# The last pair's first two products interleaved, an opening rewritten, and when the corner sums run

## The chip, the cores and the metric

The kernel runs on one core of a Trainium2 chip. The metric is the device time of one execution in microseconds (us); lower is better. The engines are named as the profile names them: PE (TensorE; PEld is its weight load), DVE (VectorE), ACT (ScalarE), POOL (GpSimd), SP (SyncE, here only a DMA queue).

## The reference

A decayed linear attention over 4 batches, 8 heads, 768 positions and head size 64, in fp32, feeds a feed-forward layer on 3072 tokens:

```python
# per block of 64 positions (the kernel uses 128, which is the same function)
intra = (qb @ kb^T) * Dmask            # Dmask[i, j] = lam^(i-j) for i >= j, else 0
out   = intra @ vb + (qb * lam^(i+1)) @ kv_state
kv_state = lam^block * kv_state + (kb * lam^(block-1-j))^T @ vb
# then, on x = out as [3072 tokens, 512]
h = x @ w_in                           # 512 -> 2048
g = where(h > 0, h, exp(min(h, 0)) - 1)   # ELU
y = g @ w_out                          # 2048 -> 512
```

## The kernel before

**Tiling.** A block g is 128 positions of one batch; there are 24 (6 chunks in time x 4 batches, g = 4 x chunk + batch). Blocks 0 to 3 stand alone; from 4 on they go in pairs (4 and 5, up to 22 and 23), named by the first. Per block the attention has these steps, each a letter of the order that is written out by hand: `T` transposes q and k (on PE with copies by DVE and ACT; from block 8 on with DMA transposes on SP), `S` the scores, whose mask is multiplied in on DVE as two `pp` tiles, `P` the block's output (psO, copied to xt), `U` the update of the state, `z`/`Z` its zeroing, `M` the decay of the old state (stt), `W` the transposes, `kd` (the decayed keys, on POOL) and `M` of a later block together.

**The feed-forward.** `1:g:j` (function `mm1`) is one block of the first product: 8 or 16 matmuls into one of two psH banks, then exp and relu on ACT and later one instruction on DVE (L640) that makes g, the ELU, and so frees the psH bank. `2:g:j` (function `mm2`) is a plain second product. From pair 8 on the second product of a pair is done with seven products instead of eight, M1 to M7, as in Strassen's scheme: `7:g:i` (function `mm2_seven`) runs them in the order M3, M4, M5, M2, M1, M7, M6, each 8 matmuls of 256 columns, one for each pair of slices of the 2048. Their operands are the g tiles themselves (gg; M3 and M4), sums of gg's quarters (fp for M5 and M2, fe for M1, fd for M7 and M6; function `sums`, L497 on POOL or L500 on DVE as `SHARED` says) and sums of w_out (wf; functions `w_sums`, `F` on DVE and `G` on POOL). M3, M5, M1 and M6 write one psM bank of the pair, M4, M2 and M7 the other (M5 adds onto M3's half, M2 onto M4's, M6 onto M1's); the next pair takes the two banks the other way round. The products are combined at the corners: ACT copies M3 and M4 out (L558), POOL adds them (t, L594), ACT copies M5 and M2 out (L569), POOL makes u (L605) and s2 (L565), DVE adds M1 to u (w1, also L565), and DVE makes the last two quarters of the output with M7 and M6 (osb, L582). The last pair's output is stored in four pieces, each as soon as it is there.

**What sets the order.** The program's order is each engine's order. Until pair 6 it is the string `OPEN`; POOL's loads and other work of that time follow `POOL_ORDER` (q, k, v, i and o are loads of q, k, v, w_in and w_out, d is kd, m is M). After that, a loop puts one `1:` block after the other and between them the seven products of the pair before and, at fixed offsets (`AT`), the attention of the pair to come; `LAGU` says how far behind plain second products may fall before they go two at a time. `BANKS` gives the PSUM banks of single steps; two names are two banks. DVE's work is deferred through lists: `pending` (the g of the last `1:` block), `late` (masks, state updates, corner sums), `slow` (the sums of gg) and `later` (the osb of M7 and M6). `flush`, called at the head of every product, emits the pending g, then at most one of `late` and of `slow`, then what is due in `later`:

```python
while later and later[0][0] <= 0:
    later.pop(0)[1]()
```

In `mm2_seven` the products 2, 4 and 5 first empty `slow`; product 6 first empties `late` until w1 is made.

Of the kernel before, what the change touches and what calls it, by code (L numbers as in the profile page):

```python
# [11 lines left out]
ALU = mybir.AluOpType  # L12
# [3 lines left out]
def kernel(  # L16
# [11 lines left out]
    nc = tc.nc  # L28
# [3 lines left out]
    L = 128  # L32
# [14 lines left out]
        "q1 k0 iota k2 k1 q2 v0 v1 i0 i1 v2 i3 i2 o0 o1 d0 k3 q3 i4 i5 d1 o2 d2 o3 d3 o4 v3 o5 "  # L47
        "i6 i7 k4 o7 o6 q4 k6 m4 v4 q6 d5 d4 q8 q10 k8 d6 v6 v8 d7 v10 k10 m6"
# [11 lines left out]
    )  # L60
    LAGU = 13
    LATE = 4
    MACT = 12
    DELAY = 0
# [3 lines left out]
    SHARED = {8: 'D', 10: 'ED', 12: 'ED', 14: 'ED', 16: '', 18: '', 20: '', 22: 'ED'}  # L68
    AT = {'L': -19, 'l': 1, 'W': -13, 'T': -5, 'S': -7, 'B': -5}
    BANKS = (  # L70
        "S0=M0,A S1=D,C S2=D,M1 S3=D,B P0=M1 P1=M0 P2=B P3=A U0=B U1=B U2=B U3=M1 T0=M1,D "
        "T1=D,C T2=M0,D T3=B T4=B T5=D T6=M1 T7=D M2=C M3=M0"
# [449 lines left out]
    def mm2_seven(g0, i):  # L522
        flush()
        while slow and i in (2, 4, 5):
            slow.pop(0)()
# [4 lines left out]
        while i == 6 and "w1" not in z:  # L530
            late.pop(0)()
# [8 lines left out]
        out = z["bank1" if m in (4, 2, 7) else "bank0"][:, half]  # L540
        for s in range(NFT // 2):
            t = g2[(g0, s // 2)]
            p, d, e = forms[(g0, s // 2)]
            u = s % 2
            lhs = {3: t[:, u, 0, 0, :], 4: t[:, u, 1, 1, :], 1: e[:, u, :], 7: d[:, u, 1, :],
                   6: d[:, u, 0, :], 5: p[:, u, 0, :], 2: p[:, u, 1, :]}[m]
            if m in (5, 2):
                rhs = wo16[s][:, 1, R_] if m == 5 else wo16[s][:, 0, L_]
            else:
                rhs = wf[s][:, (3, 4, 1, 6, 7).index(m), :]  # L550
            nc.tensor.matmul(  # L551
                out, lhsT=lhs, rhs=rhs, start=(s == 0 and m in (3, 4, 1, 7)),
                stop=(s == NFT // 2 - 1), skip_group_check=True,
            )

        def keep(n):
            z[n] = msb.tile([128, 256], FP32, tag=n, bufs=1, name=f"{n}_{g0}")
            nc.scalar.copy(out=z[n][:], in_=out)  # L558
# [13 lines left out]

        last = g0 == NG - 2
# [15 lines left out]
        if m == 3:  # L589
            keep("m3")  # L590
        elif m == 4:
            keep("m4")
# [15 lines left out]
        elif m == 2:  # L608
            corner(1, L_)
            if COMB is nc.vector:  # L610
                late.insert(0, lambda: comb("s2", "t", None, ALU.subtract))
            else:
                comb("s2", "t", z[1][:, L_], ALU.subtract)
        elif m == 1:
            late.insert(0, lambda: comb("w1", "u", None, ALU.add, nc.vector))
        elif m == 7:
            last_of(0, L_, "w1", ALU.subtract)
        else:
            last_of(1, R_, "s2", ALU.add)
# [6 lines left out]
    def flush():  # L626
        while pending:
# [19 lines left out]
            if g0 in SEVEN and j % 2 == 1:  # L647
                slow.extend(sums(g0, j // 2))
        if late:
            late.pop(0)()  # L650
        if slow and len(late) < 2:
            slow.pop(0)()
# [211 lines left out]
```

## Time and profile before

| | us |
|---|---|
| median of 14 runs | 213.59 |
| lowest and highest of them | 213.07, 214.87 |
| the profiled execution's own time | 214.82 |
| its span, first to last instruction | 213.1 |
| PE busy in it | 197.6 (93%) |
| POOL, DVE, ACT busy | 160.2, 159.2, 137.9 |
| M1 to M7 of a pair, each | 0.87 from the first matmul to the next product's |

In the lines of a timeline the columns are start, duration, engine, source line, operation, output<-inputs, shapes and count; the brackets give the idle time of the engine just before and what ended it. Matmuls are pipelined: eight of 256 columns that take 1.03 to the end of the last let the next start after 0.87. DVE's and ACT's instructions overlap their neighbours by some 0.1 us. In the chain of waits the columns are start, duration and what ran.

### The profile page before, as it was taken

Reading aid. Unit: us, or ns where it says so; the run is one execution under the profiler, and the core shown is the slowest. Engines: PE = TensorE matmul, PEld = TensorE weight load, DVE = VectorE, ACT = ScalarE, POOL = GpSimd, SP = SyncE. Lnnn points to the kernel's source line nnn. Section 1 sums busy time; section 2 is a strip of 40 time slices with the busy share of each in tenths; the row PEclk is TensorE's granted clock in tenths of the full one; section 3 lists DMA queues with packets and bytes.
Section 4 is the critical chain, followed back from the end, with each engine's and each line's share of the span. In section 5 each row is a group of like instructions: output and inputs, shape, how many; then the busy total and the mean of one; then the engine's idle time right before and its main releaser. Section 6 shows DMA issues by size and latency. Waiting matters only on the chain.

```text
span 213.1 us, 5654 instructions
## 1 busy us (share of the span) xinstructions
PE 197.6 (93%) x2224; PEld 158.2 (74%) x2224; DVE 159.2 (75%) x294; ACT 137.9 (65%) x277; POOL 160.2 (75%) x187
## 2 busy tenths in 40 slices
PE   0679999999999999999999999999999999999983
PEld 0459676777676676667887887887988878888862
DVE  3864382579975968989978879879989889886522
ACT  4535664883876675866966966867567667577630
POOL 7999599999999999597999999996361201206961
PEclk9999999999999999999999999999999999999998
DMA  8999999999993030999959959979999611011032
GB/s 88 135 172 185 197 169 174 166 177 195 134 186 87 3 98 3 123 168 143 136 84 158 121 87 154 117 95 152 111 119 179 101 52 49 3 49 49 3 115 82
DMA packets 102122, 24.61 MB, mean 116 GB/s; under 512 B 92624, under 2 KB 99280, under 8 KB 102096
## 3 DMA queue, kind: packets, MB, share of 16 engines
q0 software_dynamic: 79760, 13.50, 83.3%
q1 hardware_dynamic: 22336, 10.76, 27.2%
q8 instruction: 17, 0.28, 0.6%
q14 instruction: 9, 0.07, 0.2%
HBM read 27.27 MB, written 6.29 MB: 158 GB/s over the span
## 4 chain that ended last, share of the span: by engine, by line
PE 69%; DVE 8%; DMA 7%; ACT 7%; POOL 5%; issue 2%; SPq 0%; ACTq 0%; POOLq 0%; DVEq 0%
PE psH L674 31%; PE psM L551 20%; PE psM L699 10%; DMA wo<-in_moe_w_out_dram 5%; ACT e L680 3%; ACT psH L681 3%; PE psS L304 3%; DVE gg L640 2%; DMA kT<-kn 2%; PE psO L340 2%; DVE g L640 2%; PE psO L346 1%; POOL wi L149 1%; POOL vn L107 1%; POOL kn L107 1%
## 5 line engine op out<-in xcount | busy, mean ns | idle before, releaser
L674 PE MATMUL psH<-xt,wi 128*128 128x256 f16 (+1 forms) x896 | 101.5, 262 | 2.5 <-DVE gg L640 1.2
L674 PEld LDWEIGHTS <-wi 128*128 128x128 f16 x896 | 79.4, 100 | 17.7 <-issue 4.0
L680 ACT ACTIVATE e<-psH 128x512 f32<-128x512 f32 x96 | 57.3, 597 | 48.7 <-PE psH L674 47.7
L681 ACT ACTIVATE psH<-psH 128x512 f32<-128x512 f32 x96 | 57.0, 593 | 0.0
L640 DVE SCALAR_TENSOR_TENSOR gg<-e,psH 128x512 f16<-128x512 f32 x64 | 43.7, 683 | 16.5 <-ACT psH L681 16.2
L640 DVE SCALAR_TENSOR_TENSOR g<-e,psH 128x512 f16<-128x512 f32 x32 | 21.9, 684 | 18.1 <-ACT psH L681 17.9
L320 DVE TENSOR_TENSOR pp<-psS,mask 128x512 f16<-128x512 f32 x48 | 31.4, 683 | 3.8 <-PE psS L304 3.8
L699 PE MATMUL psM<-wo,g 128*128 128x512 f16 x128 | 32.1, 379 | 0.5 <-DMA wo<-in_moe_w_out_dram 0.5
L176 POOL TENSOR_TENSOR kd<-kn,ks 128x512 f16<-128x512 f16 x20 | 21.0, 1055 | 5.6 <-DMA kn<-in_k_dram 5.5
L497 POOL TENSOR_TENSOR fd<-gg 128x512 f16<-128x512 f16 x20 | 24.3, 1216 | 0.1
L517 POOL TENSOR_TENSOR wf<-wo 128x256 f16<-128x256 f16 (+1 forms) x28 | 21.1, 794 | 0.2
L497 POOL TENSOR_TENSOR fe<-gg 128x256 f16<-128x256 f16 x16 | 11.8, 735 | 12.0 <-DVE gg L640 11.9
L594 POOL TENSOR_TENSOR t<-m,m 128x256 f32<-128x256 f32 x8 | 5.9, 736 | 18.3 <-ACT m L558 18.3
L699 PEld LDWEIGHTS <-g 128*128 128x128 f16 x128 | 11.7, 98 | 10.3 <-issue 0.8
L551 PE MATMUL psM<-wf,gg 128*128 128x256 f16 x128 | 16.8, 273 | 0.8 <-DVE osb L582 0.5
L551 PE MATMUL psM<-wo,fp 128*128 128x256 f16 x128 | 16.5, 273 | 0.0
L551 PE MATMUL psM<-wf,fd 128*128 128x256 f16 x128 | 16.4, 273 | 0.0
L107 POOL DMA_DIRECT2D qn<-in_q_dram x13 | 14.8, 1136 | 0.9 <-POOLq L848 0.8
L107 POOL DMA_DIRECT2D kn<-in_k_dram x14 | 15.3, 1096 | 0.0
L107 POOL DMA_DIRECT2D vn<-in_v_dram x14 | 15.3, 1098 | 0.0
L500 DVE TENSOR_TENSOR fp<-gg 128x512 f16<-128x512 f16 x32 | 14.6, 456 | 0.6
L551 PEld LDWEIGHTS <-gg 128*128 128x128 f16 x128 | 11.9, 98 | 3.2 <-issue 0.7
(62 smaller groups left out, 250.4 us busy)
## 6 DMA issues: line engine op xcount, KB each, us to landing
out_dram<-osb SPq DMA_DIRECT2D x22, 256.0 KB, 2.6
kn<-in_k_dram POOLq DMA_DIRECT2D x10, 256.0 KB, 6.5
qn<-in_q_dram POOLq DMA_DIRECT2D x10, 256.0 KB, 6.0
vn<-in_v_dram POOLq DMA_DIRECT2D x10, 256.0 KB, 8.4
wi<-in_moe_w_in_dram POOLq DMA_DIRECT2D x8, 256.0 KB, 7.8
wo<-in_moe_w_out_dram POOLq DMA_DIRECT2D x8, 256.0 KB, 9.5
kn<-in_k_dram POOLq DMA_DIRECT2D x4, 128.0 KB, 4.2
vn<-in_v_dram POOLq DMA_DIRECT2D x4, 128.0 KB, 5.6
```

What stands on the lines that cost most here:

```text
L107: nc.gpsimd.dma_start(out=t[:].rearrange("p b h d -> p (b h) d"), in_=src)
L176: nc.gpsimd.tensor_tensor(out=kd[:], in0=of(kg, g), in1=ks[:].unsqueeze(2).broadcast_to([128, H, 64]), op=ALU.mult,)
L320: nc.vector.tensor_tensor(out=P[:], in0=pts[hh][:], in1=mask[:, hh::2, :], op=ALU.mult)
L497: nc.gpsimd.tensor_tensor(out=out[:], in0=in0, in1=in1, op=op)
L500: lambda out=out, in0=in0, in1=in1, op=op: nc.vector.tensor_tensor(out=out[:], in0=in0, in1=in1, op=op)
L517: eng.tensor_tensor(out=out, in0=in0, in1=in1, op=op)
L551: nc.tensor.matmul(out, lhsT=lhs, rhs=rhs, start=(s == 0 and m in (3, 4, 1, 7)), stop=(s == NFT // 2 - 1), skip_group_check=True,)
L640: nc.vector.scalar_tensor_tensor(out=g.rearrange("p f c t -> p (f c t)"), in0=e[:], scalar=-1.0, in1=r[:], op0=ALU.add, op1=ALU.min,)
L674: nc.tensor.matmul(pH[:, f * n * 128 : (f + 1) * n * 128], lhsT=wi16[i][:, kk, w * 128 : (w + 1) * 128], rhs=xg[g0][:, kk, :], start=(kk = ...
L680: nc.scalar.activation(e[:], pH[:], AF.Exp)
L681: nc.scalar.activation(pH[:], pH[:], AF.Relu)
L699: nc.tensor.matmul(psM[g][:, cols], lhsT=gts[(g, j * FB + f)], rhs=wo16[i][:, w, cols], start=first and f == 0, stop=end and f == FB - 1, ...
```

## The change

- In `mm2_seven`, of the last pair (22): M3 runs 7 of its 8 matmuls as product 0. Product 1 begins with `SPLIT` = 3 matmuls of M4, then M3's last and its copy by ACT, then M4's other five.
- The osb of the pair ahead is emitted before the last g: product 6 of pair 20 calls no `flush`, and product 0 of pair 22 first empties `later`.
- `slow` holds its pair beside each entry, and products 2, 4 and 5 empty only what belongs to their own pair.
- w1 is emitted with M1 and no longer put in `late`.
- `SHARED`: pair 8's fe goes from DVE to POOL (four instructions).
- `OPEN`, `POOL_ORDER`: steps change places. `BANKS`: T1's second half goes to bank D, where its first is, and no longer to C. `LAGU` is 14 instead of 13 and T's offset -7 instead of -5.

On PE the built order differs in these places only: T3 ahead of 1:0:1, S3 ahead of 1:0:2, U2 ahead of 1:3:2, 1:4:2 ahead of S6 and S7, and the last pair's M3 and M4. On DVE, the masks of S6 go behind the g of 1:4:3, the fe of pair 8 are gone, in each pair one state update goes ahead of the second fp and w1 ahead of fe and fd, and at the end the osb of pair 20's M6 goes ahead of the last g. On SP one store goes behind the two transposes of block 10.

```diff
@@ -44,32 +44,33 @@
     WI = [2] * 8
     WO = [2] * 8
     POOL_ORDER = (
-        "q1 k0 iota k2 k1 q2 v0 v1 i0 i1 v2 i3 i2 o0 o1 d0 k3 q3 i4 i5 d1 o2 d2 o3 d3 o4 v3 o5 "
-        "i6 i7 k4 o7 o6 q4 k6 m4 v4 q6 d5 d4 q8 q10 k8 d6 v6 v8 d7 v10 k10 m6"
+        "q1 k0 iota k2 k1 q2 v0 v1 i0 i1 v2 i3 i2 o0 d0 o1 k3 q3 i4 i5 d1 o2 d2 o3 d3 o4 v3 o5 "
+        "i6 i7 k4 o7 o6 q4 k6 m4 v4 q6 d5 d4 q10 k8 q8 d6 v6 d7 v8 v10 m6 k10"
     )
     RAW = "q0"
     FIRST = "q0:0 c0 c1 c2"
     OPEN = (
-        "z3 z0 z1 Z2 Z1 z2 Z0 T0 T1 S0 S1 T2 P0 P1 S2 1:0:0 U0 1:1:0 P2 1:1:1 1:2:0 2:0:0 "
-        "1:2:1 2:1:0 1:0:1 T3 2:2:0 1:0:2 S3 1:2:2 2:2:1 U1 1:1:2 2:1:1 2:0:1 P3 2:0:2 1:3:0 "
-        "2:1:2 1:1:3 M 1:2:3 Z3 2:2:2 1:3:2 U2 1:3:1 2:1:3 1:0:3 T4 T5 2:2:3 1:3:3 S4:5 2:3:0 "
-        "2:0:3 2:3:2 U3 F0 B:P4:P5:U4:U5 M 2:3:3 1:4:1 T6 1:4:0 G3 T7 2:3:1 G4 W9 1:4:3 G5 G1 "
-        "S6:7 1:4:2 G2 2:5:0 2:4:0 1:4:4 1:4:5 W8 B:P6:P7:U6:U7 1:4:7 1:6:1 2:5:1 2:4:1 G7 "
-        "1:4:6 1:6:0 G6 2:4:2 S8:9 1:6:2 1:6:4 2:5:2 2:5:3 W11 1:6:3 1:6:6 B:P8:P9:U8:U9 1:6:7 "
-        "2:4:3 1:6:5 W10 L12"
+        "z1 z0 Z1 z3 z2 Z2 Z0 T0 T1 S0 S1 T2 P0 P1 S2 1:0:0 U0 1:1:0 P2 1:1:1 1:2:0 2:0:0 "
+        "1:2:1 2:1:0 T3 1:0:1 2:2:0 S3 1:0:2 1:2:2 2:2:1 U1 1:1:2 2:1:1 2:0:1 P3 2:0:2 1:3:0 "
+        "2:1:2 1:1:3 1:2:3 Z3 2:2:2 U2 1:3:2 1:3:1 M 2:1:3 1:0:3 T4 T5 2:2:3 1:3:3 S4:5 2:3:0 "
+        "2:0:3 2:3:2 U3 F0 B:P4:P5:U4:U5 M 2:3:3 1:4:1 T6 1:4:0 G3 T7 2:3:1 G4 W9 1:4:3 G1 G5 "
+        "1:4:2 S6:7 2:5:0 2:4:0 G2 1:4:4 1:4:5 W8 B:P6:P7:U6:U7 1:4:7 1:6:1 2:5:1 2:4:1 1:4:6 "
+        "G7 1:6:0 G6 2:4:2 S8:9 1:6:2 1:6:4 2:5:2 2:5:3 W11 1:6:3 1:6:6 B:P8:P9:U8:U9 1:6:7 "
+        "2:4:3 W10 1:6:5 L12"
     )
-    LAGU = 13
+    LAGU = 14
     LATE = 4
     MACT = 12
+    SPLIT = 3
     DELAY = 0
     COMB = nc.gpsimd
 
     SEVEN = (8, 10, 12, 14, 16, 18, 20, 22)
-    SHARED = {8: 'D', 10: 'ED', 12: 'ED', 14: 'ED', 16: '', 18: '', 20: '', 22: 'ED'}
-    AT = {'L': -19, 'l': 1, 'W': -13, 'T': -5, 'S': -7, 'B': -5}
+    SHARED = {8: 'ED', 10: 'ED', 12: 'ED', 14: 'ED', 16: '', 18: '', 20: '', 22: 'ED'}
+    AT = {'L': -19, 'l': 1, 'W': -13, 'T': -7, 'S': -7, 'B': -5}
     BANKS = (
         "S0=M0,A S1=D,C S2=D,M1 S3=D,B P0=M1 P1=M0 P2=B P3=A U0=B U1=B U2=B U3=M1 T0=M1,D "
-        "T1=D,C T2=M0,D T3=B T4=B T5=D T6=M1 T7=D M2=C M3=M0"
+        "T1=D,D T2=M0,D T3=B T4=B T5=D T6=M1 T7=D M2=C M3=M0"
     )
     TAGS = {w: t.replace(",", " ") for w, t in (x.split("=") for x in BANKS.split())}
 
@@ -520,15 +521,18 @@
     later, sides = [], [0, 1]
 
     def mm2_seven(g0, i):
-        flush()
-        while slow and i in (2, 4, 5):
-            slow.pop(0)()
+        last = g0 == NG - 2
+        if last and i == 0:
+            while later:
+                later.pop(0)[1]()
+        if g0 != NG - 4 or i < 6:
+            flush()
+        while i in (2, 4, 5) and any(x[0] == g0 for x in slow):
+            slow.pop(0)[1]()
         if i == 0:
             seven[g0] = {}
             sides.reverse()
         z = seven[g0]
-        while i == 6 and "w1" not in z:
-            late.pop(0)()
         if i < 2:
             while later:
                 later.pop(0)[1]()
@@ -537,25 +541,47 @@
             )
         m = (3, 4, 5, 2, 1, 7, 6)[i]
         half = L_ if i < 4 else R_
-        out = z["bank1" if m in (4, 2, 7) else "bank0"][:, half]
-        for s in range(NFT // 2):
-            t = g2[(g0, s // 2)]
-            p, d, e = forms[(g0, s // 2)]
-            u = s % 2
-            lhs = {3: t[:, u, 0, 0, :], 4: t[:, u, 1, 1, :], 1: e[:, u, :], 7: d[:, u, 1, :],
-                   6: d[:, u, 0, :], 5: p[:, u, 0, :], 2: p[:, u, 1, :]}[m]
-            if m in (5, 2):
-                rhs = wo16[s][:, 1, R_] if m == 5 else wo16[s][:, 0, L_]
-            else:
-                rhs = wf[s][:, (3, 4, 1, 6, 7).index(m), :]
-            nc.tensor.matmul(
-                out, lhsT=lhs, rhs=rhs, start=(s == 0 and m in (3, 4, 1, 7)),
-                stop=(s == NFT // 2 - 1), skip_group_check=True,
-            )
-
-        def keep(n):
+
+        def place_of(m):
+            return z["bank1" if m in (4, 2, 7) else "bank0"][:, half]
+
+        def keep(m):
+            n = f"m{m}"
             z[n] = msb.tile([128, 256], FP32, tag=n, bufs=1, name=f"{n}_{g0}")
-            nc.scalar.copy(out=z[n][:], in_=out)
+            nc.scalar.copy(out=z[n][:], in_=place_of(m))
+
+        def terms(m, slices):
+            for s in slices:
+                t = g2[(g0, s // 2)]
+                p, d, e = forms[(g0, s // 2)]
+                u = s % 2
+                lhs = {3: t[:, u, 0, 0, :], 4: t[:, u, 1, 1, :], 1: e[:, u, :],
+                       7: d[:, u, 1, :], 6: d[:, u, 0, :], 5: p[:, u, 0, :],
+                       2: p[:, u, 1, :]}[m]
+                if m in (5, 2):
+                    rhs = wo16[s][:, 1, R_] if m == 5 else wo16[s][:, 0, L_]
+                else:
+                    rhs = wf[s][:, (3, 4, 1, 6, 7).index(m), :]
+                nc.tensor.matmul(
+                    place_of(m), lhsT=lhs, rhs=rhs,
+                    start=(s == 0 and m in (3, 4, 1, 7)),
+                    stop=(s == NFT // 2 - 1), skip_group_check=True,
+                )
+
+
+        end = NFT // 2
+        if last and i == 0:
+            terms(3, range(end - 1))
+            return
+        if last and i == 1:
+            terms(4, range(SPLIT))
+            terms(3, [end - 1])
+            keep(3)
+            terms(4, range(SPLIT, end))
+        else:
+            terms(m, range(end))
+        out = place_of(m)
+
 
         def comb(n, x, y, op, eng=COMB):
 
@@ -587,9 +611,9 @@
 
 
         if m == 3:
-            keep("m3")
+            keep(3)
         elif m == 4:
-            keep("m4")
+            keep(4)
             z["t"] = msb.tile([128, 256], FP32, tag="t", bufs=1, name=f"t_{g0}")
             nc.gpsimd.tensor_tensor(
                 out=z["t"][:], in0=z["m3"][:], in1=z["m4"][:], op=ALU.add
@@ -612,7 +636,7 @@
             else:
                 comb("s2", "t", z[1][:, L_], ALU.subtract)
         elif m == 1:
-            late.insert(0, lambda: comb("w1", "u", None, ALU.add, nc.vector))
+            comb("w1", "u", None, ALU.add, nc.vector)
         elif m == 7:
             last_of(0, L_, "w1", ALU.subtract)
         else:
@@ -645,11 +669,11 @@
                 for c in range(n):
                     gts[(g0 + c, j * (FB // n) + f)] = g[:, f, c, :]
             if g0 in SEVEN and j % 2 == 1:
-                slow.extend(sums(g0, j // 2))
+                slow.extend((g0, x) for x in sums(g0, j // 2))
         if late:
             late.pop(0)()
         if slow and len(late) < 2:
-            slow.pop(0)()
+            slow.pop(0)[1]()
         for x in later:
             x[0] -= 1
         while later and later[0][0] <= 0:
```

More of the change, by code (lines that the diff above doesn't have):

```diff
@@ L571, in corner @@
                 store(c, half)
-        last = g0 == NG - 2
         def store(c, cols):
```

## The prediction

> **What bounds the kernel now.** I read the page's busy shares first, then the chain that ended last, then the timelines at the places that the diff touches. The share and the chain both say TensorE:
>
> ```profile
> PE 197.6 (93%) x2224; PEld 158.2 (74%) x2224; DVE 159.2 (75%) x294; ACT 137.9 (65%) x277; POOL 160.2 (75%) x187
> PE 69%; DVE 8%; DMA 7%; ACT 7%; POOL 5%; issue 2%; SPq 0%; ACTq 0%; POOLq 0%; DVEq 0%
> ```
>
> From 99 to 191 us TensorE does the same 15.5 us per pair over and over, with one gap of 0.37 us in each (PE waits for a g to free a psH bank; the chain there is exp, relu, g). A change pays only where TensorE waits. Two such places matter here. The first is the end, in the timeline of all engines:
>
> ```profile
> 202.23 0.93 PE L551 MATMUL psM<-wf,gg 128*128 128x256 f16 x7
> 202.74 0.69 DVE L640 SCALAR_TENSOR_TENSOR gg<-e,psH 128x512 f16<-128x512 f32 x1 [0.73 <-ACT psH L681]
> ...
> 203.48 0.28 PE L551 MATMUL psM<-wf,gg 128*128 128x256 f16 x1 [0.32 <-DVE gg L640]
> ...
> 203.80 0.41 DVE L582 TENSOR_TENSOR osb<-t,psM 128x256 f32<-128x256 f32 x1
> ...
> 204.27 1.03 PE L551 MATMUL psM<-wf,gg 128*128 128x256 f16 x8 [0.51 <-DVE osb L582]
> ```
>
> Seven slices of M3 run, the eighth waits for the last g, and M4 waits for DVE's corner sum of pair 20 (L582), which stands behind that g and its fp on DVE. Matmuls of this shape start 0.109 us apart (8 in 0.87), so TensorE was free at 202.23 + 0.76 = 202.99 and at 203.48 + 0.11 = 203.59: it loses 0.49 + 0.68 = 1.17 us. After 204.27 it runs 48 matmuls without a gap.
>
> The second place is the written-out opening. The timelines of TensorE and DVE there show:
>
> ```profile
> 42.39 1.07 PE L674 MATMUL psH<-xt,wi 128*128 128x128 f16 x16
> ...
> 56.33 0.68 DVE L640 SCALAR_TENSOR_TENSOR g<-e,psH 128x512 f16<-128x512 f32 x1
> ...
> 57.09 0.40 PE L304 MATMUL psS<-qT,kT 64*128 64x128 f16 x8 [0.43 <-ACT kT L293]
> 57.41 1.05 PE L674 MATMUL psH<-xt,wi 128*128 128x256 f16 x8
> ...
> 98.17 0.92 PE L304 MATMUL psS<-qT,kT 64*128 64x128 f16 x16
> ```
>
> and the chain of waits in order of time shows what ends the opening:
>
> ```profile
> 94.09 4.56 DMA kT<-kn
> 98.65 0.05 issue
> 98.70 0.40 PE psS L304 x8
> ```
>
> S13's eight score matmuls wait for the transposed keys of block 13. Elsewhere 16 such matmuls take 0.56 us (113.97 to 114.53), so S13 could have started at 98.17 + 0.28 = 98.45: TensorE has 0.25 us of slack there, and whatever the opening loses is forgiven up to that.
>
> **What the Trainium skill says.** "PSUM — Partial Sum Buffer", Terms: two engines may not use one bank and quadrant at the same time, reads included. The trace agrees: kT7's copy on ACT starts at 56.44, when qT7's on DVE, of the same bank, ends (55.72 + 0.69). "Advanced Engine Details and Errata", GPSIMD Details: Pool shares SBUF interfaces with DVE and conflicts with DVE instructions that have two SBUF inputs. The trace agrees: DVE's fe takes 0.28 us alone, and 1.23 at 94.37 while Pool issues a load (94.11 to 95.33). "TensorE: Matmul & The Clock Gate", Part 1: the clock is raised after a busy window of about 3.4 us. The trace fits: 128-column matmuls are 0.107 us apart at 16.97 (16 in 1.91) and 0.055 at 23.37 (16 in 1.05).
>
> **The change part by part.**
>
> *The end.* The built order on DVE is now: osb of M7, osb of M6, last g, fp. M6's last matmul starts at 201.36 + 7 x 0.109 = 202.12 and ends 0.28 later, so the sum runs 202.44 to 202.85. The g is behind it; its own input is there at 202.70, so it starts at 202.86 (0.12 later than before) and ends at 203.55. TensorE: M3's seven slices to 202.99; bank free since 202.9, so three slices of M4 to 203.32; M3's last slice at 203.60; the other five of M4 from 203.71 to 204.26. M5 adds onto M3's bank, so it waits for ACT's copy of M3: the slice ends 203.88, the copy follows 0.10 later (203.86 against 203.76 before) and takes 0.37, so M5 starts at 204.39. Before, M5 started at 204.27 + 0.87 = 205.14. **Gain 0.75.** It holds to the end only if Pool keeps up. Pool: fe 203.62 to 204.53, fd to 205.66, t to 206.42, u to 207.15. DVE's M1 sum 207.20 to 207.62, and M6, which adds onto M1's bank, starts at 204.39 + 4 x 0.87 = 207.87: 0.25 to spare. The four stores keep their order and sizes behind the last sums. Bounds: 0.60 if the copies or Pool add 0.15, 0.83 if M5 needn't wait.
>
> *U2 ahead of 1:3:2.* U2's four matmuls and the switch take 0.24, so 1:3:2 starts at 39.62 instead of 39.38, its exp at 40.77, relu done 41.85, g 41.87 to 42.56. The second psH block after it starts at 42.39 before, exactly when that g (41.65 to 42.34) frees the bank; it now starts at 42.60. U2's old place didn't cost it, since 1:3:1 waits for another g (39.89 to 40.58) either way. **Loss 0.21.**
>
> *1:4:2 ahead of S6 and S7.* psH has two banks. 1:4:2 needs the one that the g of 1:4:0 frees, at 57.02 (first row of DVE above). TensorE is free at 56.15 and now idles to 57.06; before, S6 ran in this time. The wait for kT7 at 57.09 goes, but 1:4:2 (0.96 to the switch) and 16 score matmuls (0.56) after 57.06 end at 58.58, against 58.30 before. **Loss 0.28.** On DVE the g of 1:4:3 comes ahead of the masks of S6; it waits for ACT until 58.5, and the masks end by 62.4 against 61.02; P7 needs the last at about 62.8. Hidden, with 0.4 left.
>
> *T1 in one bank.* T1's key transposes (8.65) now wait for qT1, which ends at 8.45 + 0.69 = 9.14, so S0 and all behind it move by 0.55. Hidden twice: the first psH block waits 0.30 at 15.71 for wi (the matmuls ahead of it fit until then), and a product waits 0.52 at 22.94 for wo. Between 0 and 0.3 if this cover is thinner than it looks.
>
> *T3 and S3 one step earlier.* T3's inputs have landed (kd3 reads the keys at 23.81; the queries were loaded 0.9 us behind them). The same TensorE work, no psH wait: 0.
>
> *Pool's loads.* kd0 goes ahead of wo_1's load (1.0 us later in issue); wo_1 lands 10.5 us after issue, in a backlog of DMA, so its landing stays. q8 and k8, d7 and v8, k10 and m6 swap: k10's load is issued some 2.9 us later, still in the backlog; the blocks' score matmuls are at 69.59 and 82.74, several us after their transposes. On SP one store moves behind the transposes of block 10, which start some 7 us earlier: nobody waits. 0.
>
> *fe of pair 8 to Pool.* DVE sheds 0.28 + 0.58 + 1.23 + 1.24 = 3.3 us, but the psH at 97.21 waits for a g (96.47) that itself waits for ACT, so TensorE gains nothing. Pool gets 4 x 0.66 = 2.6; it idles 2.76 before 90.97 and 1.23 before 101.32, so one fe is free and it runs about 0.75 late from there to pair 14. The next loads go out up to 1.3 us late; their transposes landed at 109.08 for score matmuls at 113.97. Hidden by 4.9 us. 0.
>
> *A product waits for its own pair's sums only, M1's sum at once.* In each pair DVE's M1 sum moves ahead of fe and fd, and a state sum ahead of fp. The state sum waits for ACT (103.80 + 1.69 = 105.49), 0.3 of the 0.55 us that DVE idles before the next g. 0. LAGU and the offset of T move no instruction.
>
> Sum: -0.75 + 0.21 + 0.28 - 0.25 (slack) = **-0.51 us**. The profiled execution took 214.82 (span 213.1 and 1.7 around it), so it becomes 214.3, span 212.6. It lies 1.2 above the median of the runs, 213.59; the same difference gives 213.1. About 0.3%, 0.64 us, is what a measurement of this kernel can tell from no change.
>
> **The rivals.** (1) The opening's losses do not show: keys 13 may land earlier, since Pool's next load, which shared the DMA engines with them, starts 0.7 later, or another wait covers them. For it: both losses rest on psH banks freed within 0.05 us. Against: nothing between 57 and 97 waits for anything but TensorE's own results. Then -0.75 to -1.0, 212.7. (2) Slower: TensorE's clock. T1's wait opens a gap of 0.8 us at 8.4; if the activity window then misses and the clock rises one window (3.4 us) after about 20.8, TensorE runs at half speed into 24.2 and loses 1.7, less 0.52 of slack: +1.2, in all +0.7, 214.3. It decides only if the clock rises after about 22. Against: 16.54 to 22 stays packed, since it hangs on the landing at 15.71. (3) The slack at 98.45 is not there, or M5 gains 0.6 alone: -0.1 to -0.25, 213.4. (4) The end does not do what it says, M4's three slices holding M3's last: they are through at 203.32, before the g; I give it nothing apart.
>
> **Chances.** Forecast 0.45 (within 0.3%), rival 1 0.40 (faster by more), rival 3 0.05 (within), rival 2 0.10 (slower). So faster 0.40, within 0.50, slower 0.10. The range 212.4 to 213.9 takes rivals 1 and 3 whole; the likeliest case's own is 212.8 to 213.4.
>
> **What would show it.** After: M4 x3 ahead of M3's last slice, then gaps of about 0.28 and 0.13 on TensorE where 1.17 were; a gap of 0.9 ahead of 1:4:2 near 57 and none for kT7; S13 some 0.25 later than 98.70; last osb at 209.3. If the last osb less S13's time has not shrunk by 0.75, the end is wrong; if S13 comes at 98.5 or earlier, the opening is; if 128-column matmuls are still 0.107 apart at 22 us, it is the clock.

## The result and the profile after

The change made the kernel slower: 217.63 us, median of 10 runs (216.78 to 220.05), against 213.67 of the kernel before (48 runs, 212.79 to 215.06); ratio 1.0181, 95% interval 1.0159 to 1.0204. The forecast was 213.1, with 0.10 for slower. In several kernels of this study, never in the kernel before, of which no run is above 215.29, the runs fall into two groups some 4 us apart, and the ratios leave an upper group out as disturbed; so counts stand beside the medians.

The profiled execution of after took 215.11 (span 213.3). Its page, with the group of DVE's `fp`, and then that group on the page of before:

```profile
PE 196.7 (92%) x2224; PEld 157.6 (74%) x2224; DVE 161.7 (76%) x290; ACT 137.9 (65%) x277; POOL 162.8 (76%) x191
PE 68%; DVE 13%; ACT 10%; POOL 4%; issue 3%; ACTq 0%; POOLq 0%; DVEq 0%
L501 DVE TENSOR_TENSOR fp<-gg 128x512 f16<-128x512 f16 x32 | 19.9, 623 | 0.6
```

```profile
L500 DVE TENSOR_TENSOR fp<-gg 128x512 f16<-128x512 f16 x32 | 14.6, 456 | 0.6
```

DVE's share of the chain went from 8% to 13%, and it works longer with four instructions fewer: the same 32 fp take 5.3 us more. Of that, 1.85 are in one fp; six others take 0.70 to 1.29 where they took 0.42 to 0.70. The chain of waits of after, in order of time, shows the one that TensorE waits for (start, duration, what ran):

```profile
98.75 1.20 DVE pp L321 x2
...
101.06 2.42 DVE fp L501
103.48 0.61 DVE pp L321
104.09 0.04 issue
104.14 0.22 PE psO L341
```

The timeline of POOL there, and the two rows of TensorE around the wait:

```profile
98.50 1.15 POOL L108 DMA_DIRECT2D vn<-in_v_dram  x1
99.66 0.69 POOL L498 TENSOR_TENSOR fe<-gg 128x256 f16<-128x256 f16 x1
100.30 1.17 POOL L498 TENSOR_TENSOR fd<-gg 128x512 f16<-128x512 f16 x1
101.41 0.68 POOL L498 TENSOR_TENSOR fe<-gg 128x256 f16<-128x256 f16 x1
102.04 1.15 POOL L498 TENSOR_TENSOR fd<-gg 128x512 f16<-128x512 f16 x1
103.15 0.91 POOL L618 TENSOR_TENSOR t<-m,m 128x256 f32<-128x256 f32 x1
```

```profile
102.65 0.22 PE L341 MATMUL psO<-pp,vn 128*64 128x128 f16 x1
104.14 0.22 PE L341 MATMUL psO<-pp,vn 128*64 128x128 f16 x1 [1.26 <-DVE pp L321]
```

The same place before, POOL and DVE:

```profile
101.32 0.66 POOL L497 TENSOR_TENSOR fe<-gg 128x256 f16<-128x256 f16 x1 [1.23 <-DVE gg L640]
101.69 0.57 DVE L500 TENSOR_TENSOR fp<-gg 128x512 f16<-128x512 f16 x1
```

One fp, 0.57 us at this place before, takes 2.42, while POOL runs an fd, an fe and an fd without a pause; before, POOL had paused for 1.23 us just ahead of it. Behind it on DVE stands the last mask of block 13, and for that P13 holds TensorE for 1.26 us.

The end of after, TensorE with DVE and ACT:

```profile
201.53 1.04 PE L698 MATMUL psH<-xt,wi 128*128 128x256 f16 x8
...
203.27 2.16 PE L565 MATMUL psM<-wf,gg 128*128 128x256 f16 x16
203.53 0.42 DVE L606 TENSOR_TENSOR osb<-t,psM 128x256 f32<-128x256 f32 x1 [0.48 <-POOL fd L498]
203.87 0.68 DVE L664 SCALAR_TENSOR_TENSOR gg<-e,psH 128x512 f16<-128x512 f32 x1
...
204.98 0.86 ACT L551 COPY m<-psM 128x256 f32<-128x256 f32 x2 [1.23 <-PE psM L565]
205.40 1.91 PE L565 MATMUL psM<-wo,fp 128*128 128x256 f16 x16
...
210.02 0.42 DVE L606 TENSOR_TENSOR osb<-t,psM 128x256 f32<-128x256 f32 x1 [0.45 <-PE psM L565]
```

M3 and M4 now run as sixteen matmuls within 2.16 us. From the start of the last psH block to that of the last osb it is 210.02 - 201.53 = 8.49 us; before it was 209.76 - 200.49 = 9.27:

```profile
200.49 1.04 PE L674 MATMUL psH<-xt,wi 128*128 128x256 f16 x8
...
209.76 0.42 DVE L582 TENSOR_TENSOR osb<-t,psM 128x256 f32<-128x256 f32 x1 [0.45 <-PE psM L551]
```

The opening of after, at the places of the prediction:

```profile
28.28 0.89 PE L698 MATMUL psH<-xt,wi 128*128 128x128 f16 x13 [0.31 <-DVE g L664]
...
56.61 1.05 PE L698 MATMUL psH<-xt,wi 128*128 128x256 f16 x8 [0.50 <-DVE g L664]
...
98.03 0.62 PE L305 MATMUL psS<-qT,kT 64*128 64x128 f16 x16
```

The wait for kT7 is gone and 1:4:2 waits for its g instead; S13's scores (in the last row) wait for nothing any more. The wait at 28.28 was not foreseen.

In the profiled executions the last psH block starts 1.04 us later in after than in before, and the end takes 0.78 of it back; the medians differ by 3.96. The clock tells a part of it: the profiled execution has a mean TensorE clock of 1.000, ten of the eleven others 0.984 to 0.992. It is also 2.5 us below the median, and none of after's slower runs has a profile, so what happens in them is read from the experiments.

### The profile page after: what moved, and what is told of

The parts are those of the page before. It is cut to its first block, busy times and chain, and to the rows that moved or that the text cites. A ratio compares the mean times of both kernels' runs of the same rounds, so it can differ in the third digit from the quotient of the medians.

```text
span 213.3 us, 5656 instructions
## 1 busy us (share of the span) xinstructions
PE 196.7 (92%) x2224; PEld 157.6 (74%) x2224; DVE 161.7 (76%) x290; ACT 137.9 (65%) x277; POOL 162.8 (76%) x191
## 4 chain that ended last, share of the span: by engine, by line
PE 68%; DVE 13%; ACT 10%; POOL 4%; issue 3%; ACTq 0%; POOLq 0%; DVEq 0%
PE psH L698 30%; PE psM L565 17%; PE psM L723 11%; ACT e L704 4%; ACT psH L705 4%; DVE gg L664 3%; DVE g L664 3%; PE psS L305 3%; PE psO L341 3%; DVE pp L321 2%; PE psO L347 2%; PE psT L286 1%; POOL fe L498 1%; DVE qT L293 1%; DVE fp L501 1%
## 5 line engine op out<-in xcount | busy, mean ns | idle before, releaser
L498 POOL TENSOR_TENSOR fe<-gg 128x256 f16<-128x256 f16 x20 | 14.4, 720 | 11.6 <-DVE gg L664 10.5
L501 DVE TENSOR_TENSOR fp<-gg 128x512 f16<-128x512 f16 x32 | 19.9, 623 | 0.6
L341 PE MATMUL psO<-pp,vn 128*64 128x128 f16 x192 | 12.6, 230 | 1.3 <-DVE pp L321 1.3
```

Of the source, the lines that this page charges most:

```text
L498: nc.gpsimd.tensor_tensor(out=out[:], in0=in0, in1=in1, op=op)
L501: lambda out=out, in0=in0, in1=in1, op=op: nc.vector.tensor_tensor(out=out[:], in0=in0, in1=in1, op=op)
```

## The experiments

Two theories. **POOL theory:** pair 8's fe fill POOL's pauses, POOL then runs back to back, and DVE's fp, with two SBUF inputs, can't get at SBUF; everything behind it on DVE is late. **Opening theory:** the new opening costs more than forecast, and the rest is a consequence. The runs of one batch share the runs of before (213.61 to 213.79, medians).

### The parts alone

**e1_end**: only the end (shortened).

```diff
+        if last and i == 0:            # later first; M3's slices 0 to 6
+        if last and i == 1:            # M4 x3, M3's last and its copy, M4 x5
+        if g0 != NG - 4 or i < 6: flush()
```

> The kernel before with the last pair alone changed: M4's three matmuls ahead of M3's last, and the osb of pair 20's M6 ahead of the last g. All theories: the profile of the changed kernel shows 8.5 us from the last psH block to the last osb where the kernel before takes 9.3, so 0.75 faster, 212.9 against 213.65. If instead the end itself costs time in most runs, it is slower than before.

Measured: 212.81 (211.76 to 213.56), ratio 0.9936 (0.9916 to 0.9955). The end gains 0.9 us in the medians; its trace has the same 8.49 us behind the last psH block as after.

**e2_fe8**: only pair 8's fe on POOL.

```diff
-    SHARED = {8: 'D', ...
+    SHARED = {8: 'ED', ...
```

> The kernel before with pair 8's four fe on Pool instead of DVE, nothing else. Pool theory (Pool then runs fe and fd without a break, DVE's fp with its two SBUF inputs is starved for over 2 us, the last mask of block 13 comes late and P13 waits, 1.26 us in the one profile there is): at least 1 us slower, up to the whole 4 if most runs have more such waits. Opening theory (the loss is in the written-out opening): within 0.5 of before.

Measured: 217.58; 13 of 16 runs lie at 216.68 or above, three at 214.26 to 214.85. Four instructions moved by one letter give nearly the whole loss, and this time the profiled execution is one of the slower runs. Its timeline of DVE, TensorE's row behind it, and a table of stretches (stretch, length, busy time of the five engines; the third column from the right is the granted clock):

```profile
99.39 4.18 DVE L500 TENSOR_TENSOR fp<-gg 128x512 f16<-128x512 f16 x1
103.49 0.68 DVE L320 TENSOR_TENSOR pp<-psS,mask 128x512 f16<-128x512 f32 x1
```

```profile
104.22 0.22 PE L340 MATMUL psO<-pp,vn 128*64 128x128 f16 x1 [3.02 <-DVE pp L320]
```

```profile
103.00:105.40 2.40, 1.18 (x35) 1.10 (x35) 2.40 (x5) 0.37 (x1) 0.28 (x1) 1.00 0.60 113
105.40:108.80 3.40, 3.40 (x18) 2.34 (x17) 2.24 (x4) 0.80 (x2) 2.64 (x3) 0.50 0.25 88
108.80:112.00 3.20, 3.20 (x31) 2.86 (x30) 1.55 (x3) 2.12 (x5) 1.98 (x3) 1.00 0.01 3
```

fp lasts until POOL's run (fd, fe, fd, t, kd, 98.71 to 103.28) is over, P13 waits 3.02 us, and 1.2 us after that wait TensorE's clock is halved for some 3.4 us, which costs 1.7 more. One such stretch in a span of 215.8 makes a mean clock of 1 - 1.7/215.8 = 0.992: nine of e2_fe8's 16 runs show this value, and nine of after's 12 lie at 0.990 to 0.992.

**e3_open**: only the new OPEN, POOL_ORDER, BANKS, LAGU and AT (as in the diff above).

> The kernel before with the changed opening alone: the new OPEN, POOL_ORDER, BANKS, LAGU and offset of T. Pool theory: within 0.7 of before (the two lost psH waits of 0.2 and 0.3 at most). Opening theory: 3 to 5 us slower, with a clock that rises a window later or drops for one window[...], or a wait near 20 us.

Measured: 215.24 (214.45 to 215.49), ratio 1.0050 (1.0028 to 1.0071); clock 0.999 or 1.0 in all. So the opening costs 1 to 1.5 us, more than the 0.24 forecast, but no run shows a half clock and the trace no stall: the opening theory explains a part only.

**e4_fe8dve**: after with pair 8's fe back on DVE (`8: 'D'`).

> The changed kernel with pair 8's fe put back on DVE. Pool theory: the loss is gone, at or below before (213.0 to 213.7). Opening theory: still 3 us or more slower, 216.5 to 217.7.

Measured: 215.72; five of 12 runs at 213.71 to 214.23, seven at 215.35 to 219.34. Neither theory expected this: there is a second cause. In its trace it is a pair later (DVE, TensorE, and the stretch of the half clock):

```profile
116.89 3.45 DVE L501 TENSOR_TENSOR fp<-gg 128x512 f16<-128x512 f16 x1
```

```profile
120.99 0.22 PE L341 MATMUL psO<-pp,vn 128*64 128x128 f16 x1 [2.30 <-DVE pp L321]
```

```profile
122.10:125.50 3.40, 3.40 (x18) 2.44 (x17) 3.00 (x5) 0.68 (x2) 2.63 (x3) 0.50 0.51 138
```

**f3_code**: all code edits with every constant of before.

> All code edits of the change (the end, own-pair sums, M1's sum at once) with every constant of before (opening, POOL_ORDER, BANKS, SHARED, LAGU, AT). Pool theory: the loss is with pair 8's fe, so this equals the end alone, 212.4 to 213.2, though the state sum that now goes ahead of fp makes one fp a pair last 1.3 us instead of 0.5 without a wait of TensorE. Per-pair theory (own-pair sums and M1 at once put fp against POOL's fd): fp of 1.3 us or more makes a g or a mask late in every pair, 0.3 us for each of seven, total 214 to 215.5.

Measured: 213.06; eight of 12 runs at 211.93 to 213.35, four at 215.45 to 217.47. In the profiled one (215.45) fp at 115.88 takes 3.45 us and P waits 2.30, without a half clock. Without constants the code brings the end's gain and, in a third of the runs, a stall. Which of the per-pair edits does it is settled by k1_sum below: it differs from e4_fe8dve in one line, that of "own pair's sums", and has no stall. How is not shown. The line puts a state sum ahead of the last fp of a pair, and that fp, at 104.83, takes 1.40 (0.70 at 105.18 before); but the long one comes 11 us later, and its place in DVE's order is the old one. What differs around it is POOL: before, it pauses 0.22 ahead of an fe at 116.65; here it doesn't pause.

### Is it POOL?

**f1_fe0**: one of the four fe moved.

```diff
-            if w in SHARED.get(g0, ""):
+            if w in SHARED.get(g0, "") or (g0, jj, w) == (8, 0, "E"):
```

> The kernel before with only the first of pair 8's four fe moved from DVE to POOL (0.66 us of POOL work, inside the 2.76 us that POOL idles before 90.97). Pool theory (moving all four uses up POOL's idle time, POOL then runs its instructions back to back and DVE's fp, which has two SBUF inputs, is starved for 2 to 4 us): no fp over 1.5 us, P13 waits under 0.3 us as before, no half clock, total within 0.3% of before (213.1 to 214.3). Order theory (any fe of pair 8 that leaves DVE pulls the fp ahead, onto POOL's instructions, whatever POOL has left of idle time): fp of 2 us or more at about 99 to 101, total 215 or more.

Measured: 213.41, ratio 1.0 (0.9981 to 1.0018); none of 20 runs over 214.51, fp 0.57 at 100.04.

**f2_lag**: DVE's work as before, POOL's more by three instructions whose results are unused.

```diff
+            if w == "D" and g0 == 8 and jj > 0:
+                x = msb.tile([128, 2, 128], FP16, tag="extra", ...)
+                nc.gpsimd.tensor_tensor(out=x[:], in0=t[:, :, 0, 0], in1=t[:, :, 1, 1], op=ALU.add)
```

> The kernel before, DVE's work unchanged, with three additional POOL instructions of fe's size (128x256 out, results unused) where pair 8's fd of jj 1 to 3 are issued; it adds to POOL alone about what the moved fe add. Pool theory: POOL's lag alone starves a DVE fp by 2 us or more between 98 and 122, P13 or a P of pair 12 waits 1 to 3 us, often with a half clock behind it; total 214.7 to 218. Order theory (it takes the fe away from DVE, so that the fp comes early): nothing starves since DVE's order is as before, total within 0.3% (213.1 to 214.3).

Measured: 217.52; 15 of 20 runs at 216.53 or above, 12 of them with a clock of 0.989 or 0.992; five at 213.47 to 214.53. The profiled one was of the lower five; there an fp takes 2.17 at 96.23, but where nobody waits long for it. DVE lost no work here, so the order theory falls. No profile of a slower run of this kernel exists; that they lose what e2_fe8 loses is inferred from their times and clocks.

**g1_fd8**: pair 8's fe on POOL, its fd on DVE in exchange (`8: 'E'`).

> The kernel before with pair 8's four fe on POOL, as in e2_fe8, and pair 8's four fd on DVE in exchange. POOL then has less to do in pair 8 than before (4 x 0.66 in, 4 x 1.16 out), DVE a little more. Pool theory (POOL's backlog starves fp): no fp over 1.5 us between 98 and 104, P13 waits under 0.3 us, no half clock, total 213.1 to 214.3. Order theory (fe gone from DVE pulls the fp onto POOL's instructions): fp of 2 us or more again, total 215 to 218.

Measured: 213.79, ratio 1.0004 (0.9984 to 1.0023); one of 12 runs at 218.45. With all four fe on POOL but less POOL work in all, the loss is gone, nearly always.

### The opening taken apart

**f4_t1**: e3_open with T1 in two banks again (`T1=D,C`).

> The new opening, POOL_ORDER, LAGU and AT over the kernel before, as in e3_open (215.24), but with T1 in banks D and C as before. If T1's one bank costs what the trace of e3_open shows at 20 us (TensorE about 0.5 us later, with no cover left): 214.5 to 214.9. If the prediction's cover holds (T1 hidden): no change against e3_open, 215.0 to 215.5, and the loss is all in T3, S3, U2 and 1:4:2.

Measured: 214.82, ratio 1.0058 (1.0038 to 1.0078), against 1.0050 for e3_open. The medians differ by 0.4, the ratios point the other way: T1's share isn't settled.

**g2_nots**: and with T3 and S3 in their old places.

```diff
-        "1:2:1 2:1:0 T3 1:0:1 2:2:0 S3 1:0:2 ...
+        "1:2:1 2:1:0 1:0:1 T3 2:2:0 1:0:2 S3 ...
```

> f4_t1 (214.82) with T3 and S3 also back in their old places, so that of the opening's changes those of U2, 1:3:2 and 1:4:2 remain, with POOL_ORDER, LAGU and AT. If T3 and S3 cost what the trace of e3_open shows at 26.6 to 28.3 (0.5 us): 214.1 to 214.4. The prediction's 0 for T3 and S3: no change, 214.6 to 215.0. The prediction's sum for what remains (0.21 + 0.28, less 0.25 of slack or not): 213.8 to 214.1.

Measured: 214.01, ratio 1.0007 (0.9992 to 1.0023). T3 and S3 cost 0.8 us by the medians. The traces say 0.66: from the start of 1:2:1, the psH block ahead of both, to U1's it is 30.41 - 23.37 = 7.04 us in before and 7.04 here, 7.69 in f4_t1, 7.70 in e3_open and after. The timeline of g2_nots has no wait there: S3 starts at 26.92, the psH block at 27.25 and a second product at 28.16, each as TensorE comes free.

**k1_sum**: after without the two suspects (`8: 'D'`, and all of `slow` emptied again).

```diff
-        while i in (2, 4, 5) and any(x[0] == g0 for x in slow):
+        while slow and i in (2, 4, 5):
```

> The change without its two suspects: pair 8's fe back on DVE, and products 2, 4 and 5 empty the whole of slow again (so DVE's order in a pair is that of before). What remains is the new opening and the end. If the account closes, e3_open's +1.1 to +1.5 and e1_end's -0.9 add up: 213.8 to 214.7, no run over 215.5 and no half clock. If a further cause is in the opening itself (a stall or a half clock that came with the sooner end), 215.5 or more.

Measured: 213.78 (213.35 to 215.08), ratio 1.0011 (0.9990 to 1.0031). All runs have a clock of 0.998 or above. The opening and the end cancel. What after loses beyond that, 217.63 - 213.78 = 3.85 us, is the two suspects'. Against e4_fe8dve, 215.72, only the line of `slow` is changed: with it, seven of 12 runs were at 215.35 or above, without it none.

### Why does fp wait through several POOL instructions?

Here the extra work stands behind the kernel's own (e1_end), so only the duration of fp in it is read.

**g3_side**: POOL's four instructions wait for nothing, for ACT copies long done, or for late ones; DVE runs PSUM products and fp.

> The end alone, with extra work behind the kernel's own: six groups in which DVE runs one or two PSUM products, an fp, a PSUM product and a second fp, while POOL runs four subtractions of fd's size that start together with them. Groups 1 and 2: POOL's instructions wait for nothing; 3 and 4: they wait for ACT copies that ended long before; 5 and 6: each waits for an ACT copy of the one before, so POOL has gaps of 0.4 us or more. Starving theory (DVE's two-input instruction gets in only when POOL has a gap): fp lasts until the end of POOL's run in groups 1 to 4, 2 to 4 us, and at most 1.5 us in 5 and 6. Turn-taking theory (DVE waits for the instruction that POOL is in, then goes first): fp lasts at most 1.2 + 0.4 = 1.6 us in all groups. The PSUM products, with one SBUF input, stay at 0.68 us in either.

Measured: fp 0.41 to 1.06 in groups 1 to 4, 0.41 to 1.35 in 5 and 6; PSUM products 0.68. DVE is let in at the next boundary between two POOL instructions, whether POOL has gaps or not. The starving theory falls in this form.

**g4_when**: the kernel's own sequence of fe, fd, t and one of kd's size, eight times of arrival each.

> The end alone, with extra work behind the kernel's own: 24 groups of one fp on DVE against a run of POOL instructions that wait for nothing. In groups 1 to 8 POOL runs subtractions of fd's size only, in 9 to 16 fe, fd, fe, fd, fe, fd, t and one of kd's size (the order in which fp was held up for 4.18 us), in 17 to 24 the same without the first fd; in each eight, DVE's fp arrives at eight different times, some 0.15 us apart. Kind theory (a short fe behind an fd keeps DVE out): waits of one instruction, 1.2 us at most, in groups 1 to 8, of two or more instructions, 2 to 4 us, in most of 9 to 24. Moment theory (what counts is the point at which fp arrives in POOL's instruction): long and short ones in each eight, long ones at the same arrival times. Neither, if all 24 last at most 1.6 us: then it takes something that only the kernel's middle has (TensorE, ACT and the DMAs at work), and stays open.

Measured: 0.41 to 1.25 in all 24.

**g5_dma**: with DMA issues by POOL ahead.

> The end alone, with extra work behind the kernel's own: twelve groups of one fp on DVE, arriving at four times, against the POOL run fe, fd, fe, fd, t and one of kd's size. In groups 1 to 4 two fd stand ahead of that run; in 5 to 8 two DMA issues on POOL (loads of k and v, results unused); in 9 to 12 the same two issues, and then an fe that waits some 1 us for ACT. In the kernels every fp that was passed over stood behind DMA issues on POOL without a pause since. DMA theory (after DMA issues POOL keeps the shared interface over instruction boundaries, until it next pauses): fp lasts at most 1.3 us in groups 1 to 4 and 9 to 12, and 2 to 4 us in 5 to 8. If all twelve stay under 1.6 us, DMA issues are not what it takes, and it stays open.

Measured: 0.41 to 1.23 in all twelve.

**g6_busy**: with TensorE, ACT, DMA transposes and loads at work.

> The end alone, with extra work behind the kernel's own: sixteen groups of one fp on DVE, arriving at four times, against a run of eight or more POOL instructions without a pause. Beside it run in groups 1 to 4 matmuls and ACT copies, in 5 to 8 four DMA transposes on SP, in 9 to 12 two loads issued by POOL ahead of its run, in 13 to 16 all of these. Company theory (fp is passed over when something else of the kernel's middle loads SBUF): waits of 2 us or more in one of the four kinds and in the last. If all sixteen stay under 1.6 us, the long wait is not reproduced outside the kernel's middle, and what decides it stays open.

Measured: 0.41 to 1.25 in all sixteen. None of these three brought the long wait back.

**g7_skew**: two fe on a part of the partitions ahead of the run.

```diff
+                r = slice(0, 32) if kind != "H" else slice(0, 64)
+                nc.gpsimd.tensor_tensor(out=fs[1 + x][2][r], in0=t[r, :, 0, 0], in1=t[r, :, 1, 1], op=ALU.add)
```

> The end alone, with extra work behind the kernel's own: sixteen groups of one fp on DVE, arriving at four times, against the POOL run fe, fd, fe, fd, t and one of kd's size. Ahead of that run stand two fe on all partitions in groups 1 to 4, on partitions 0 to 31 in 5 to 8, on partitions 0 to 63 in 9 to 12; in 13 to 16 two on partitions 0 to 31 and then one that waits for ACT. The Trainium skill, GPSIMD Engine Reference, 2.1 Instruction dispatch, says that POOL's eight cores, 16 partitions each, are not held together from one instruction to the next. Drift theory (cores with nothing to do go ahead, so from then on there is no moment between two instructions at which all leave the shared interface, until POOL waits): fp lasts at most 1.3 us in groups 1 to 4 and 13 to 16, and 2 to 4 us in 5 to 12. If all sixteen stay under 1.6 us, drift of this kind does not do it, and it stays open.

Measured: 0.65 to 1.30 in groups 1 to 4; **5.32 to 6.32 in all of 5 to 12**, each time to the end of POOL's run, longer than the 2 to 4 expected; 0.49 to 0.91 in 13 to 16, where POOL waits once after the partial instructions. Groups 4 and 5 in the timelines of DVE and POOL:

```profile
238.93 0.71 DVE L926 TENSOR_TENSOR fp<-gg 128x512 f16<-128x512 f16 x1
...
246.94 6.31 DVE L926 TENSOR_TENSOR fp<-gg 128x512 f16<-128x512 f16 x1
```

```profile
245.33 1.28 POOL L913 TENSOR_TENSOR fe<-gg 32x256 f16<-32x256 f16 x2
246.57 0.66 POOL L883 TENSOR_TENSOR fe<-gg 128x256 f16<-128x256 f16 x1
247.20 1.14 POOL L880 TENSOR_TENSOR fd<-gg 128x512 f16<-128x512 f16 x1
```

The rows of POOL look like those of the other groups; only the 32 partitions of the first differ.

**g8_sync**: e2_fe8, and ahead of the third and fourth fe of a pair on POOL two small instructions, of which the second waits for the first.

```diff
+                    nc.gpsimd.tensor_tensor(out=sync[0][:], in0=ident16[:, 0:2], in1=ident16[:, 0:2], op=ALU.add)
+                    nc.gpsimd.tensor_tensor(out=sync[1][:], in0=sync[0][:], in1=sync[0][:], op=ALU.add)
```

> e2_fe8 (all four fe of pair 8 on POOL) with two small POOL instructions (128x2) more ahead of the third and fourth fe of each pair whose fe are on POOL; the second reads what the first writes and so waits until all of POOL's cores are through with the first. It adds work to POOL, 0.2 to 0.4 us each time. Drift theory (POOL's cores have drifted apart after the DMA issues, and fp finds no moment between two instructions until they are together again): no fp over 1.5 us between 98 and 122, no wait of P13 over 0.3 us, no half clock, total 213.1 to 214.5 in at least nine of ten runs. Backlog theory (POOL without idle time is enough, whatever its cores do): POOL is later still, fp held up for 2 to 4 us as in e2_fe8, total 215 to 218.

Measured: 214.32, where e2_fe8 has 217.58; clock 0.998 or above in all 17 runs, 15 of them under 215.5, no fp over 1.15. A little above what the theory gave, since 10 of 17 runs, not nine of ten, are at 214.5 or below; what delays the two slowest, 216.13 and 216.61 at full clock, is open. Work added to POOL without a wait had the opposite effect in f2_lag. The same two instructions without the wait between them were not run, so that it is the wait is inferred from g7_skew.

**g9_after_sync**: the same two instructions in the changed kernel, nothing undone.

> The changed kernel itself with the same two small POOL instructions ahead of the third and fourth fe of each pair whose fe are on POOL, nothing else undone. Drift theory: the whole of the main loss goes, and what remains is what k1_sum has (213.78), 213.4 to 214.4, fp about 0.5 us in the mean. Backlog theory: as the changed kernel, 216.8 to 218.5.

Measured: 215.81 (215.40 to 216.50), clock 0.998 or above, against 217.63. In the timelines of POOL, DVE and TensorE at the place of after's stall:

```profile
99.49 0.21 POOL L502 TENSOR_TENSOR sync<-ident 128x2 f16<-128x2 f16 x1
99.78 0.19 POOL L505 TENSOR_TENSOR sync<-sync 128x2 f16<-128x2 f16 x1
...
100.57 1.14 POOL L508 TENSOR_TENSOR fd<-gg 128x512 f16<-128x512 f16 x1
101.68 0.84 POOL L508 TENSOR_TENSOR fe<-gg 128x256 f16<-128x256 f16 x1
```

```profile
100.63 1.36 DVE L511 TENSOR_TENSOR fp<-gg 128x512 f16<-128x512 f16 x1
```

```profile
102.65 0.22 PE L341 MATMUL psO<-pp,vn 128*64 128x128 f16 x1 [0.21 <-DVE pp L321]
```

fp comes in 0.06 us into an fd, with no pause of POOL near, and is let in at that fd's end; the fe that follows is longer for it (0.84 against 0.66). The long stalls are gone in the changed kernel itself. It missed the forecast of 213.4 to 214.4 all the same: fp's mean is 724 ns, and P waits 0.21 to 0.38 us for a mask behind it in each of four pairs. TensorE loses 0.37 + 0.54 + 0.54 + 0.53 = 2.0 us there, counting the step it could have taken, about the distance to k1_sum, 2.03.

No run beats e1_end, 212.81, the end alone.

## Why the prediction was wrong, step by step

**"fe of pair 8 to Pool ... 0" failed, and with it the forecast.** The arithmetic of POOL's time was about right: it runs without its pauses from about 91 on, and its kd behind t starts 0.55 us later after M3 than before (5.45 against 4.90), forecast 0.75. The step went on to look only at what POOL itself feeds, loads and transposes ("hidden by 4.9 us"). It had just cited that POOL conflicts with DVE's instructions of two SBUF inputs, and had a row in which DVE's fe took 1.23 instead of 0.28, but did not ask which DVE instruction would meet POOL once the pauses were gone. It was fp, with block 13's mask behind it and P13 behind that. Price: 3.02 us of TensorE in e2_fe8's trace, 1.26 in after's, and in most runs, by their clocks, 1.7 for a half clock.

The mechanism goes further than a shared interface. The Trainium skill, "GPSIMD Engine Reference", 2.1 Instruction dispatch, says that POOL's eight cores, each with 16 partitions, aren't held together from one instruction to the next, and that where order matters a wait for an instruction's completion, which is that of all eight cores, has to stand between two. Our runs agree: behind two instructions on a part of the partitions only, fp waits to the end of the run in eight groups of eight (5.3 to 6.3 us); behind whole ones it waits for one instruction (1.35 at most in g3_side to g7_skew); and a wait brings this back, in g7_skew and in the kernel (g8_sync, g9_after_sync). That the cores had drifted in after itself is inferred from what the two small instructions did; no view shows it. What set them apart there stays open: DMA issues by POOL stood ahead of every fp of 2 us or more in the kernels' traces, but alone they did nothing in g5_dma. That it varies from run to run would explain the two groups of times.

**"A product waits for its own pair's sums only ... 0" failed.** The step asked whether the state sum that comes ahead of fp makes the next g late. It didn't. A later fp, whose order hadn't changed, met a POOL run without a pause: this is so in the one profile that f3_code and e4_fe8dve have each, and, going by the times, in four and seven of their 12 runs. How the state sum leads to it stays open.

**"T3 and S3 one step earlier ... 0" failed**, by 0.66 us in the traces, 0.8 in the medians (f4_t1 against g2_nots). The step looked at when the inputs had landed. But S3 now stands closer behind its key copy and waits for ACT (0.11), and the psH block two steps on waits 0.31 for a g: the same kind of wait that was worked out for U2 and not looked for here. (These are idle times. From start to start S3 comes 0.28 and the block 0.47 later than without a wait, and S3 had waited 0.08 in its old place.)

**T1, "hidden twice", is open.** TensorE's wait of 0.78 at 9.20 is in after's trace. Two covers were named from an execution in which weights came late (0.52 at 22.94); in e3_open it shows as a wait of 0.41 for a g at 20.61, in f4_t1 of 0.07 at 20.87, and the totals don't tell.

**U2 was right; 1:4:2 and the slack were read from one execution.** From the psH block at 37.62 to that at 42.39 it was 4.77 us before and is 5.00 in after: 0.23, forecast 0.21. At 1:4:2 TensorE waits 0.50 for the g, not 0.91, and from the psH block ahead to the product behind it is 3.07 against 3.02: 0.05, forecast 0.28. But kT7's wait, 0.43 in the profile of before, is 0.19 or 0.20 in six of the seven other traces with the old opening, and against e2_fe8's 2.78 the loss is 0.29. The slack of 0.25 at S13 varies too: in four of these seven the scores don't wait for the keys. The sum of the three, 0.24, fits g2_nots, which costs 0.15 (-0.17 to 0.49, from the ratio and 213.6), but is not shown by it. S13 came at 98.03, and by the prediction's own sign (98.5 or earlier) its opening is wrong; that sign is no clean test, since 98.70 held waits of 0.30 and 0.52 for weights that after doesn't have.

**The end was right.** Forecast 0.75; 9.27 - 8.49 = 0.78 in the trace, 0.9 in e1_end's medians. POOL kept up.

**The rivals.** The slower one, the clock rising a window later in the opening, did not occur in after's trace, where 16 matmuls of 128 columns take 1.07 at 18.96 already. A half clock did decide, but in the middle, behind a stall nobody had priced. Together: k1_sum, with the forecast's -0.51 and the T3 and S3 that it missed, stands at 0.0 to 0.2 against before; the two steps that it set to nothing add 3.85. That the opening's loss and the end's gain nearly cancel is chance. The chance of 0.10 for slower was hung on one mechanism, while three moves were costed at nothing from one view each.

## What to carry to other kernels

Work moved to POOL is paid for by DVE as well: ask which DVE instructions with two SBUF inputs come while POOL runs without a pause, what is queued behind them on DVE, and who waits for that. If such an instruction lasts several POOL instructions, a small POOL instruction that waits for the one before it bounded the wait to one instruction here; leaving POOL its pauses costs less (213.8 against 215.8). A stall of some 2 to 3 us on TensorE can cost 1.7 us more through its clock, so compare the clock of all runs and not only of the profiled one.

## What the hardware showed that I had not expected

- An fp of 0.42 us took 2.42, 3.45, 4.18 and, behind two POOL instructions on 32 partitions, 6.31 us. DVE's products of PSUM and SBUF stayed at 0.68 beside the same POOL work.
- TensorE's clock fell to half for 3.4 us after waits of 3.02 (e2_fe8) and 2.30 us (e4_fe8dve), each amid dense matmuls, and not after another of 2.30 (f3_code). The clock records of the traces say why. The changes of the clock lie whole multiples of 3.413 us apart: 26, 1 and 31 in e2_fe8, 31, 1 and 27 in e4_fe8dve, 58 in f3_code. On that grid the window just ahead of each half clock has TensorE idle for 2.25 us (101.97 to 105.38) and 2.30 us (118.69 to 122.10); f3_code's wait is cut by a boundary at 118.23 into 0.55 and 1.75. So what counts in these traces is TensorE's idle time within one window of a fixed grid: 1.75 of 3.41 us cost nothing, 2.10, in g6_busy (238.83 to 242.24), already did. The Trainium skill, "TensorE: Matmul & The Clock Gate", says in Part 1 that the window of 3.4 us runs freely, and the traces agree; in Why this matters for your kernels it advises to keep gaps under about 3 us, and a gap of 2.30 was enough once here.
